# Scores and outputs read six heads where the products are written; two heads are gathered

## Chip, cores and metric

The kernel runs on one core of one Trainium2 chip. The metric is the device time of one execution in microseconds (us). TensorE (PE) multiplies, VectorE (DVE) and ScalarE (ACT) do the elementwise work, GpSimd (POOL) small elementwise work and indexed transfers, and SyncE (SP) issues most of the DMAs, one after another in a fixed order.

## Reference, cut to what matters

Inputs are float32. A gated linear attention over 4 batches, 8 heads, 768 positions and 48 channels per head feeds a mixture of experts that routes each token to one expert, and then a second layer with a maximum of three products.

```python
for t in range(S):
    ar, ai = (a_re_n[:, :, t, :, None], a_im_n[:, :, t, :, None])
    new_re = ar * S_re - ai * S_im
    new_im = ar * S_im + ai * S_re
    kv = np.einsum('bhd,bhe->bhde', k[:, :, t], v[:, :, t])
    S_re, S_im = (new_re + kv, new_im)
    y[:, :, t] = np.einsum('bhd,bhde->bhe', q[:, :, t], S_re)
...
expert_idx = np.argmax(logits, axis=1)
...
h = np.maximum(x[mask] @ w1[e], 0.0)
out[mask] = gate_w[mask, None] * (h @ w2[e])
...
h = np.maximum(np.maximum(x @ w1, x @ w2), x @ w3)
return (h @ w_out).astype(np.float32)
```

## The kernel before

The 8 x 48 = 384 channels of a batch are split into 3 groups (`G`) of 128 partitions, and the 768 positions into 6 chunks (`NCH`) of 128. The work of a batch b has two parts.

`recur` (called R below; R0 to R3) runs the complex gates through all 64 half-chunk positions of all chunks at once, in 8 blocks of 8 steps. It is a chain on DVE: two dependent instructions per step (lines 202 and 215), with the preparation of later blocks and the products filled in between. The products (lines 169, 175 and 186) go into the tile `QK`, which holds keys and queries, each with a real and an imaginary part, all multiplied by gates. There is one buffer of `QK` for all batches (`qk_p`, 1 buffer).

`chunks` (called C; C0 to C3) works on the 6 chunks of a batch. In `QK` the 48 channels of one head are spread over the partitions in such a way that TensorE can't contract over them in place. So `restack` (line 326) copies all of `QK` by DMA into tiles `KQ` of 96 partitions, where a head's 48 real and 48 imaginary channels lie below each other: 18 DMAs per batch, in pieces of 1, 2 and 3 chunks. Then, for each chunk, `scores` multiplies keys by queries for each head (line 361, tile `sc`, one matmul per head with 96 rows), DVE masks the result into `sT` (line 363), and PE transposes the keys (line 371, tile `kt`) for `state` (lines 385 and 392, tile `W`). `state` gives `Z`, which four DMAs copy into `Zs` with 96 partitions (line 412). `output` adds to `y` the product of `sT` with the values (line 427) and that of the query with the state of the earlier chunks (line 430). After that come `rows` (line 504, tile `xp`), the routing on DVE and `place` (tile `rank`), and an indexed DMA writes the token's row to its expert's list in memory.

Every matmul of float32 appears in the trace as two instructions. `sc`, `kt`, `W`, `y`, `xp` and `rank` share four PSUM buffers in turn.

The first expert layer is cut into jobs, each a list of tokens of one expert that is known to be full early: seven jobs in plain float32 (numbers 0 to 6; lines 730 and 754), and then the rest (line 621 to 623), which starts with job 7. A job reads 8 weight tiles `wr` of 384 KB. Jobs 0 to 2 need the tokens of batch 0, jobs 3 to 6 those of batches 0 and 1, job 7 those of batches 0 to 2. With `GATE = 2` the weight loads of early jobs stand behind the copies of the attention in SP's order.

The program is written in the order of `SCHED`: R0, C0, two jobs, R1, C1, two and a half jobs, R2, C2 with R3, the other early jobs, two slices of job 7, C3, the rest. A scheduler that plans with its own durations then sets the order on each engine, so DVE, PE and SP work through fixed lists in which these parts are interleaved. From about 467 us on, only the expert layers are left.

## Time and profile before

| what | us |
|---|---|
| median of 3 runs (998.87 to 1001.46) | 999.44 |
| the profiled execution, its own time | 1002.36 |
| its span in the profile | 1000.7 |
| DVE busy in the span | 593.2 |
| PE busy in the span | 821.3 |

A row of a view is one instruction group, one stretch of time or one wait; times inside the profile count from the start of the span. "PEclk" is the granted TensorE clock as a share of full speed, "DMA share" the mean busy share of the 16 DMA engines.

### The profile page before, as it was taken

Reading aid. Unit: us, or ns where it says so; the run is one execution under the profiler, and the core shown is the slowest. Engines: PE = TensorE matmul, PEld = TensorE weight load, DVE = VectorE, ACT = ScalarE, POOL = GpSimd, SP = SyncE. Lnnn points to the kernel's source line nnn. Section 1 sums busy time; section 2 is a strip of 40 time slices with the busy share of each in tenths; the row PEclk is TensorE's granted clock in tenths of the full one; section 3 lists DMA queues with packets and bytes.
Section 4 is the critical chain, followed back from the end, with each engine's and each line's share of the span. In section 5 each row is a group of like instructions: output and inputs, shape, how many; then the busy total and the mean of one; then the engine's idle time right before and its main releaser. Section 6 shows DMA issues by size and latency. Waiting matters only on the chain.

```text
span 1000.7 us, 15691 instructions
## 1 busy us (share of the span) xinstructions
PE 821.3 (82%) x5490; PEld 723.4 (72%) x5490; DVE 593.2 (59%) x1596; ACT 417.1 (42%) x1045; POOL 144.6 (14%) x230
## 2 busy tenths in 40 slices
PE   1004784769778888789899999998999999999996
PEld 1002674558656776678799999997888888888886
DVE  6989599749984895345667877785232323232222
ACT  5444466336544652335556565563121212121211
POOL 7001011100120012001312222224010101010000
PEclk9999795989788979989899999999999999999999
DMA  9835943995489639942756776662020201020001
GB/s 324 150 104 123 241 130 110 238 242 164 137 269 212 198 94 292 216 131 74 242 177 210 216 215 215 208 210 69 24 64 1 64 1 64 1 64 1 32 1 35
DMA packets 94217, 139.20 MB, mean 139 GB/s; under 512 B 26434, under 2 KB 66770, under 8 KB 94130
## 3 DMA queue, kind: packets, MB, share of 16 engines
q1 hardware_dynamic: 88018, 121.27, 44.0%
q0 software_dynamic: 6112, 16.85, 6.1%
q8 instruction: 45, 0.74, 0.3%
q14 instruction: 42, 0.34, 0.1%
HBM read 93.80 MB, written 22.36 MB: 116 GB/s over the span
## 4 chain that ended last, share of the span: by engine, by line
PE 55%; DMA 20%; DVE 17%; ACT 3%; SPq 2%; issue 2%; POOL 1%; DVEq 0%; ACTq 0%; POOLq 0%
PE h L621 10%; PE h L622 10%; PE h L623 10%; DMA wr<-wm 7%; DMA KQ<-QK 5%; PE acc L621 5%; PE acc L623 5%; PE acc L622 5%; DVE T L202 3%; DMA wt<-qk 2%; DVE T L215 2%; PE h L730 2%; PE acc L754 2%; DMA ain<-a 2%; PE xp L504 1%
## 5 line engine op out<-in xcount | busy, mean ns | idle before, releaser
L865 DVE TENSOR_TENSOR h2s<-h,h2s 128x512 f32<-128x512 f32 x72 | 49.8, 692 | 188.2 <-PE h L623 188.2
L623 PE MATMUL h<-x2h,w2l 128*128 128x512 f32 x324 | 126.6, 391 | 0.0
L622 PE MATMUL h<-x2l,w2h 128*128 128x512 f32 x324 | 126.5, 390 | 0.0
L621 PE MATMUL h<-x2h,w2h 128*128 128x512 f32 x324 | 124.4, 390 | 0.0
L202 DVE TENSOR_TENSOR T<-gates,T 128x216 f32<-128x216 f32 x256 | 97.0, 379 | 4.7 <-ACT gates L147 0.5
L614 ACT CAST h2h<-h2s 128x512 fp32r<-128x512 f32 x36 | 22.3, 620 | 145.4 <-DVE h2s L865 145.4
L730 PEld LDWEIGHTS h<-xh,wr 128*128 128x128 f32 x336 | 51.4, 224 | 36.8 <-DMA wr<-wm 27.3
L621 PE MATMUL acc<-w2h,hh 128*110 128x384 f32 (+2 forms) x200 | 69.3, 348 | 3.9 <-ACT hh L738 3.9
L615 DVE TENSOR_TENSOR w1l<-wr,w1h 128x384 fp32r<-128x384 f32 x72 | 43.7, 607 | 47.7 <-ACT w1h L614 47.5
L623 PEld LDWEIGHTS h<-x2h,w2l 128*128 128x128 f32 x324 | 60.8, 188 | 12.8
L738 ACT ACTIVATE hh<-h 128x128 f32<-128x128 f32 (+5 forms) x128 | 45.8, 359 | 57.3 <-PE h L730 43.6
L622 PEld LDWEIGHTS h<-x2l,w2h 128*128 128x128 f32 x324 | 60.8, 188 | 12.3
L541 POOL DMA_INDIRECT xs<-x,pos x24 | 25.6, 1065 | 304.0 <-DVE T L215 74.0
L730 PE MATMUL h<-xh,wr 128*128 128x128 f32 (+1 forms) x336 | 54.7, 312 | 17.8 <-DMA wr<-wm 16.8
L621 PE MATMUL h<-xh,w1h 128*128 128x330 f32 (+3 forms) x216 | 68.1, 317 | 1.3 <-ACT xh L614 1.2
L621 PEld LDWEIGHTS h<-x2h,w2h 128*128 128x128 f32 x324 | 60.7, 188 | 11.7
L324 PE MATMUL warm_s<-QK,ones 128*128 128x480 f32 x12 | 7.3, 774 | 75.1 <-DVE QK L186 75.1
L622 PE MATMUL acc<-w2l,hh 128*110 128x384 f32 (+2 forms) x200 | 67.9, 341 | 0.0
L622 PE MATMUL h<-xl,w1h 128*128 128x330 f32 (+3 forms) x216 | 67.6, 313 | 0.0
L623 PE MATMUL h<-xh,w1l 128*128 128x330 f32 (+3 forms) x216 | 67.5, 313 | 0.0
L361 PE MATMUL sc<-KQ 96*128 96x128 f32 x384 | 54.5, 294 | 13.8 <-DMA KQ<-QK 12.6
L361 PEld LDWEIGHTS sc<-KQ 96*128 96x128 f32 x384 | 49.3, 203 | 20.3 <-issue 16.6
(204 smaller groups left out, 1967.4 us busy)
## 6 DMA issues: line engine op xcount, KB each, us to landing
wr<-wm SPq DMA_DIRECT2D x128, 384.0 KB
ain<-a SPq DMA_DIRECT2D x32, 288.0 KB
KQ<-QK SPq DMA_DIRECT2D x24, 384.0 KB
w2r<-w SPq DMA_DIRECT2D x24, 384.0 KB
xs<-zero POOLq DMA_DIRECT2D x16, 384.0 KB, 10.2
KQ<-QK SPq DMA_DIRECT2D x24, 256.0 KB
wt<-qk SPq DMA_DIRECT2D x32, 144.0 KB
pl<-qk SPq DMA_DIRECT2D x32, 144.0 KB
```

The costliest lines, as they stand in the source:

```text
L202: r = tt(out=sub(To, so, [[X, 2], [PJ, 3 * GN], [1, 2]]), in0=sub(N5, j * NW, [[1, NW]]), in1=sub(T, 2 * j, [[0, 2], [PJ, 3 * GN], [1, 2]] ...
L215: r = tt(out=new, in0=new, in1=sub(M, RW + 2 * j, [[-RW, 2], [PJ, GN], [1, 2]]), op=ALU.add)
L361: k["pe"] = nc.tensor.matmul(ps[:, i], Ks[:, h], Qs[:, h], start=True, stop=True)
L541: r = nc.gpsimd.indirect_dma_start(out=self.xs_d, out_offset=bass.IndirectOffsetOnAxis(ap=pos, axis=0), in_=x, in_offset=None, bounds_chec ...
L614: nc.scalar.copy(out=hi, in_=src)
L615: nc.vector.tensor_tensor(out=lo, in0=src, in1=hi, op=ALU.subtract)
L621: r = nc.tensor.matmul(out, ah, bh, start=first, stop=False)
L622: nc.tensor.matmul(out, ah, bl, start=False, stop=False)
L623: nc.tensor.matmul(out, al, bh, start=False, stop=last)
L730: r = nc.tensor.matmul(ps, wh[:, c], xh[:, d, :n], start=d == 0, stop=d == KD - 1)
L738: r = nc.scalar.activation(out=hh[:, :n], in_=ps, func=AF.Relu)
L865: nc.vector.tensor_tensor(out=h, in0=pss[m], in1=h, op=ALU.max)
```

## The change

On the host, channels are put on other partitions: group g of the 3 now holds the 48 channels of head 2g on partitions 0 to 47 and those of head 2g+1 on partitions 64 to 111. The 16 partitions behind each of them (48 to 63 and 112 to 127) hold a third of the channels of heads 6 and 7. `scores` and `output` read heads 0 to 5 straight from `QK`, real and imaginary part in two matmuls of 48 rows that accumulate. Heads 6 and 7 are brought together by DMA into two fixed tiles `last0` and `last1` (3 chunks each). The state `Z` is read in place, so the copies `Zs` fall away. `QK` gets a second buffer, and the rules in `recur` that kept a batch's products back (`late`) fall away. The transposes take 128 partitions instead of 96. `spread` makes `E` by one multiplication and smaller DMAs.

```diff
 def host_attn(q, k, v, a_re, a_im):
+    g, p = np.arange(G)[:, None], np.arange(128)[None]
+    own, par = p % 64 < D, p // 64
+    hh, dd = np.where(own, 2 * g + par, 6 + par), np.where(own, p % 64, 16 * g + p % 64 - D)
     def dirs(x):
-        y = x.transpose(0, 3, 1, 2).reshape(B, G, 128, NCH, C)
+        y = x.transpose(0, 1, 3, 2)[:, hh, dd].reshape(B, G, 128, NCH, C)
...
-        self.qk_p = P("a_qk", 1)
-        self.s_p = P("a_stack", 2)
+        self.qk_p = P("a_qk", 2)
+        s_p = P("a_stack", 1)
+        self.last = [s_p.tile([112, 2, 2, RC * C], F32, name=f"last{i}") for i in range(NCH // RC)]
...
-            late = b > 0 and i < 3
-            p, *more = [products(x) for x in (((), (), (0, 1))[i] if late else (i - 1,) if i else ())] or [iter(())]
+            p = products(i - 1) if i else iter(())
...
-        nc.gpsimd.memset(E, 0.0)
+        nc.gpsimd.memset(E[:, 3], 0.0)
+        nc.gpsimd.tensor_scalar(out=E[:, 0:3], in0=Ed[:112], scalar1=self.k["own"][:112], scalar2=None, op0=ALU.mult)
...
-    def restack(self, b, n, QK):
...
+    def gather(self, b, QK):
+        for lo, hi in ((0, 1), (1, RC), (RC, NCH)):
+            t, o = self.last[lo // RC], lo % RC * C
+            for g in range(G):
+                for par in range(2):
                     self.k["dma"] = self.nc.sync.dma_start(
+                        out=t[64 * par + 16 * g : 64 * par + 16 * g + 16].rearrange("p x c n -> p (x c) n")[:, :, o : o + (hi - lo) * C],
+                        in_=pview(QK, 64 * par + D, (g * NCH + lo) * C, [1, 16], [[GN * C, 4], [1, (hi - lo) * C]]),
                     )
...
+        def KQ(n, x, c, pr, par):
+            if pr == 3:
+                t, cols = last(n)
+                return t[64 * par : 64 * par + D, x, c, cols]
+            return pview(QK, 64 * par, (((x * 2 + c) * G + pr) * NCH + n) * C, [1, D], [[1, C]])
...
-                    k["pe"] = nc.tensor.matmul(ps[:, i], Ks[:, h], Qs[:, h], start=True, stop=True)
+            for pr in range(4):
+                for c in range(2):
+                    for par in range(2):
+                        k["pe"] = nc.tensor.matmul(
+                            ps[par][:, pr], KQ(n, 0, c, pr, par), KQ(n, 1, c, pr, par), start=c == 0, stop=c == 1
+                        )
...
-                    k["pe"] = nc.tensor.transpose(ps[:, i * 96 : (i + 1) * 96], Ks[:, hf * 4 + i], k["ident"][:96, :96])
+                    k["pe"] = nc.tensor.transpose(ps[:, i * 128 : i * 128 + w], x, k["ident"][:w, :w])
...
-            z = Zs[n + 1] = self.c_p.tile([96, H, D], F32, tag="Zs", name="Zs" + nm(n + 1), bufs=3)
-            for c in range(2):
-                for par in range(2):
-                    nc.sync.dma_start(
...
-                            k["pe"] = nc.tensor.matmul(o, Zf[:, h * D : h * D + m], Qs[:, h], start=False, stop=True)
+            for pr in range(4 if n else 0):
+                for c in range(2):
+                    for par in range(2):
+                        k["pe"] = nc.tensor.matmul(
+                            y[64 * par : 64 * par + D, pr], Z[n][64 * par : 64 * par + D, pr, c], KQ(n, 1, c, pr, par),
+                            start=False, stop=pr == 3 and c == 1,
+                        )
...
-SPLITS = ([(0,1),(1,3)],[(0,3)])
```

The order on the engines changes too. First DVE around the end of R3, where `QK3` is batch 3's tile, `sT_3_0_0` the masked scores of batch 3, chunk 0, and `w1l_7_0_0` the first weight slice of job 7. Before:

```order
L186 TENSOR_TENSOR QK3_2921<-qe3_2922,T_86 128x72
...
L615 TENSOR_TENSOR w1l_7_0_0_4127<-wr_7_0_0_4124,w1h_7_0_0_4126 128x384
L615 TENSOR_TENSOR w2l_7_0_0_4131<-wr_7_0_0_4124,w2h_7_0_0_4130 128x384
...
L363 TENSOR_TENSOR sT_3_0_0_4213<-sc_3_0_0_4208,mask_249 128x512
L363 TENSOR_TENSOR sT_3_0_1_4220<-sc_3_0_1_4215,mask_249 128x512
```

After:

```order
L195 TENSOR_TENSOR QK3_3052<-qe3_3053,T_86 128x72
...
L631 TENSOR_TENSOR w1l_7_0_0_4320<-wr_7_0_0_4317,w1h_7_0_0_4319 128x384
L631 TENSOR_TENSOR w2l_7_0_0_4324<-wr_7_0_0_4317,w2h_7_0_0_4323 128x384
L631 TENSOR_TENSOR w1l_7_0_1_4344<-wr_7_0_1_4341,w1h_7_0_1_4343 128x384
L631 TENSOR_TENSOR w2l_7_0_1_4348<-wr_7_0_1_4341,w2h_7_0_1_4347 128x384
L378 TENSOR_TENSOR sT_2_4_0_3703<-sc_2_4_0_3685,mask_253 128x512
L378 TENSOR_TENSOR sT_2_4_1_3705<-sc_2_4_1_3686,mask_253 128x512
```

C3 came directly behind R3; now chunks 4 and 5 of C2 stand between them.

Next PE where C3 begins, with `acc_6`, `h_4` and so on the matmuls of jobs 6 and 4. Before, all early jobs are through:

```order
L754 MATMUL acc_6_0_0_4020<-wr_6_0_6_4074,hh_6_0_6_4080 128x384
L730 MATMUL h_6_0_7_4085<-xh_6_0_4008,wr_6_0_7_4083 128x128 x3
L679 MATMUL xT_7_0_0_4110<-ident_171,xt_7_0_4105 128x120 x3
L679 MATMUL xT_7_0_1_4116<-ident_171,xt_7_0_4105 128x120 x3
L754 MATMUL acc_6_0_0_4020<-wr_6_0_7_4083,hh_6_0_7_4089 128x384
L361 MATMUL sc_3_0_0_4208<-KQ_3_0_4178 128x128 x4
L361 MATMUL sc_3_0_1_4215<-KQ_3_0_4178 128x128 x4
```

After, half of job 4 stands ahead of C3, and jobs 5 and 6 are mixed into its chunks 0 to 2:

```order
L520 MATMUL xp_2_5_4037<-idE_306,yT_2_5_4006 128x120 x4
L746 MATMUL h_4_0_4_4083<-xh_4_0_2658,wr_4_0_4_4081 128x128 x3
...
L372 MATMUL sc_3_0_0_4400<-QK3_3052 128x128
L372 MATMUL sc_3_0_1_4401<-QK3_3052 128x128
...
L746 MATMUL h_5_0_0_4132<-xh_5_0_4117,wr_5_0_0_4130 128x128 x3
L746 MATMUL h_5_0_1_4140<-xh_5_0_4117,wr_5_0_1_4138 128x128 x3
L372 MATMUL sc_3_0_1_4401<-last0_93 128x128
```

So two and a half jobs moved from ahead of C3's first scores to behind R3's end, and the two score tiles are filled in turn.

Last SP's list at the same place; `wr_6_0_7` is a weight tile of job 6, `v_3_2` the values of batch 3, chunk 2. Before:

```order
L333 DMA KQ_3_0_4178<-QK3_2921 16x16x128
L698 DMA wr_6_0_7_4083<-wm 128x768
L333 DMA KQ_3_0_4178<-QK3_2921 16x16x128 x5
L333 DMA KQ_3_0_4178<-QK3_2921 16x16x256 x6
L774 DMA x1_61<-x1o_6_0_0_4093 128x384
L333 DMA KQ_3_3_4199<-QK3_2921 16x16x384 x6
L698 DMA wr_7_0_2_4799<-wm 128x768
```

After:

```order
L714 DMA wr_7_0_0_4317<-wm 128x768
L714 DMA wr_7_0_1_4341<-wm 128x768
L339 DMA last0_93<-QK3_3052 16x4x128 x3
...
L339 DMA last0_93<-QK3_3052 16x4x256 x6
...
L366 DMA v_3_2_4534<-vs 128x384
L339 DMA last1_94<-QK3_3052 16x4x384 x6
L714 DMA wr_7_0_2_5054<-wm 128x768
L714 DMA wr_7_0_3_5084<-wm 128x768
L714 DMA wr_5_0_0_4130<-wm 128x768
```

The 18 copies remain 18, each a quarter of the size, and the weights of jobs 5 and 6 moved behind them.

## Rows read from the trace of the kernel before

**Rows 1.** Busy time by engine, from the page.
```profile
PE 821.3 (82%) x5490; PEld 723.4 (72%) x5490; DVE 593.2 (59%) x1596; ACT 417.1 (42%) x1045; POOL 144.6 (14%) x230
```
**Rows 2.** Windows: stretch, length, busy time by engine, granted clock, DMA share, GB/s.
```profile
0.00:88.00 88.00, 2.98 (x15) 2.92 (x15) 72.58 (x230) 39.24 (x100) 21.03 (x100) 1.00 0.65 175
88.00:183.00 95.00, 71.22 (x612) 58.96 (x612) 81.03 (x269) 50.96 (x141) 11.18 (x17) 0.78 0.66 165
183.00:304.00 121.00, 94.38 (x771) 75.25 (x770) 90.74 (x299) 60.90 (x178) 13.92 (x23) 0.87 0.81 212
304.00:389.00 85.00, 71.59 (x680) 60.67 (x680) 70.05 (x237) 44.78 (x128) 7.09 (x8) 0.92 0.72 187
389.00:467.00 78.00, 63.56 (x644) 53.70 (x643) 27.13 (x77) 26.40 (x75) 7.53 (x11) 0.93 0.70 165
467.00:1000.70 533.70, 517.57 (x2778) 471.86 (x2776) 251.63 (x489) 194.78 (x426) 83.82 (x74) 0.99 0.32 101
```
**Rows 3.** The same view, three stretches inside R1, R2 and R3.
```profile
135.00:182.00 47.00, 31.48 (x261) 27.10 (x260) 45.31 (x158) 26.91 (x76) 7.19 (x10) 0.71 0.45 127
225.00:267.00 42.00, 35.86 (x407) 31.93 (x406) 40.10 (x145) 27.29 (x76) 5.46 (x6) 0.91 0.53 152
328.00:367.00 39.00, 32.65 (x387) 28.24 (x386) 38.27 (x135) 24.23 (x66) 4.13 (x4) 0.94 0.52 151
```
**Rows 4.** DVE's waits from 88 to 389 us: total, times, longest.
```profile
DVE sT L363 <- PE sc L361: 21.3, 8, 5.1
DVE QK L169 <- DMA wr<-wm: 10.2, 2, 8.0
```
**Rows 5.** PE in order of time, one chunk of C3: start, length, instructions.
```profile
444.40 1.16 PE L385 MATMUL W<-v,KT 128*64 128x48 f32 x32
445.49 0.90 PE L392 MATMUL W<-Z,ident 112*112 112x384 f32 x2
446.32 0.43 PE L427 MATMUL y<-sT,v 128*64 128x128 f32 x4
446.58 0.39 PE L430 MATMUL y<-KQ,Zs 96*48 96x128 f32 x4
446.81 0.39 PE L427 MATMUL y<-sT,v 128*48 128x128 f32 x4
447.91 0.39 PE L430 MATMUL y<-KQ,Zs 96*48 96x128 f32 x4
448.23 2.05 PE L361 MATMUL sc<-KQ 96*128 96x128 f32 x16
450.11 0.82 PE L371 MATMUL kt<-ident,KQ 96*128 96x96 f32 x8
450.77 0.17 PE L531 MATMUL rank<-OH,trib 128*128 128x8 bf16 x1
451.06 1.15 PE L504 MATMUL xp<-idE,yT 112*128 112x120 f32 x8
452.14 0.68 PE L385 MATMUL W<-v,KT 128*64 128x48 f32 x16
456.17 2.05 PE L361 MATMUL sc<-KQ 96*128 96x128 f32 x16
```
**Rows 6.** PE in order of time, two slices of an early job.
```profile
384.72 0.83 PE L730 MATMUL h<-xh,wr 128*128 128x128 f32 x6
385.39 0.81 PE L754 MATMUL acc<-wr,hh 128*128 128x384 f32 x2
386.04 0.83 PE L730 MATMUL h<-xh,wr 128*128 128x128 f32 x6
```
**Rows 7.** The chain that ended last, behind R3's end and later: start, length.
```profile
398.86 10.62 DMA KQ<-QK
418.20 12.38 DMA wr<-wm
604.24 3.68 DMA wr<-wm
```

More of the change, by code (lines that the diff above doesn't have):

```diff
@@ L87, in __init__ @@
         self.T = n_p.tile([128, 6, 3 * GN, JB, 2], F32, name="T")
-        self.qk_p = P("a_qk", 1)
-        self.s_p = P("a_stack", 2)
+        self.qk_p = P("a_qk", 2)
+        s_p = P("a_stack", 1)
+        self.last = [s_p.tile([112, 2, 2, RC * C], F32, name=f"last{i}") for i in range(NCH // RC)]
+        for t in self.last:
+            self.nc.gpsimd.memset(t[32:64], 0.0)
         self.c_p = P("a_chunk", 2)
@@ L259, in recur @@
             n2 = norms[i + 2] if i + 2 < NBLK else iter(())
-            late = b > 0 and i < 3
-            p, *more = [products(x) for x in (((), (), (0, 1))[i] if late else (i - 1,) if i else ())] or [iter(())]
-            queue += [take(n1, 2), take(n2, 1), take(p, 1), take(n1, 1), take(p, 1), n1, p, *more]
+            p = products(i - 1) if i else iter(())
+            queue += [take(n1, 2), take(n2, 1), take(p, 1), take(n1, 1), take(p, 1), n1, p]
             after = THR.get(b, {}).get(i)
@@ L342, in chunks @@
         QK, Ed = self.out[b]
-        st = [self.restack(b, 0, QK)]
+        self.gather(b, QK)
+        last = lambda n: (self.last[n // RC], slice(n % RC * C, (n % RC + 1) * C))
         E = self.spread(b, Ed)
-        st += [self.restack(b, n, QK) for n in range(RC, NCH, RC)]
-        KQ = lambda n, x: st[n // RC][:, :, x, n % RC * C : (n % RC + 1) * C]
-        V, S, KTs, Z, Zs, yT = {}, {}, {}, {}, {}, {}
+        def KQ(n, x, c, pr, par):
[3 more added lines that the diff above has]
+            return pview(QK, 64 * par, (((x * 2 + c) * G + pr) * NCH + n) * C, [1, D], [[1, C]])
+        V, S, KTs, Z, yT = {}, {}, {}, {}, {}
         nm = lambda n: f"_{b}_{n}"
@@ L352, in scores @@
         def scores(n):
[L353 removed]
             V[n] = self.c_p.tile([128, DM], F32, tag="v", name="v" + nm(n), bufs=3)
             nc.sync.dma_start(V[n], v_d[b, n])
[L356 to L363 removed]
+            ps = [k["ps_m"].tile([128, 4, C], F32, tag="am", name=f"sc{nm(n)}_{par}") for par in range(2)]
+            for pr in range(4):
[4 more added lines that the diff above has]
+                        )
+            S[n] = []
+            for par in range(2):
+                s = self.c_p.tile([128, 4, C], F32, tag="sT", name=f"sT{nm(n)}_{par}", bufs=4)
+                nc.vector.tensor_tensor(out=s, in0=ps[par], in1=sub(k["mask"], 0, [[0, 4], [1, C]]), op=ALU.mult)
                 S[n].append(s)
@@ L366, in scores @@
                 return
-            KT = KTs[n] = self.c_p.tile([128, H, 2, D], F32, tag="KT", name="KT" + nm(n), bufs=1)
+            KT = KTs[n] = self.c_p.tile([128, 8, 112], F32, tag="KT", name="KT" + nm(n), bufs=1)
             for hf in range(2):
@@ L370, in scores @@
                 for i in range(4):
-                    k["pe"] = nc.tensor.transpose(ps[:, i * 96 : (i + 1) * 96], Ks[:, hf * 4 + i], k["ident"][:96, :96])
-                nc.scalar.copy(
-                    out=KT[:, hf * 4 : hf * 4 + 4].rearrange("p h c d -> p (h c d)"), in_=ps[:, 0:DM]
-                )
+                    g, c = divmod(4 * hf + i, 2)
+                    if g < G:
+                        x, w = sub(QK, ((c * G + g) * NCH + n) * C, [[1, C]]), 128
+                    else:
+                        t, cols = last(n)
+                        x, w = t[:, 0, c, cols], 112
+                    k["pe"] = nc.tensor.transpose(ps[:, i * 128 : i * 128 + w], x, k["ident"][:w, :w])
+                nc.scalar.copy(out=KT[:, 4 * hf : 4 * hf + 4], in_=sub(ps, 0, [[128, 4], [1, 112]]))
         def state(n):
@@ L1182, in body @@
             k["mask"] = mask_tile(nc, cp)
+            const("own", [128, 1])
+            nc.vector.tensor_reduce(out=k["own"], in_=sub(k["ident"], D, [[64, 2], [1, 16]]), axis=AX.XY, op=ALU.add)
+            nc.vector.tensor_scalar(out=k["own"], in0=k["own"], scalar1=-1.0, scalar2=1.0, op0=ALU.mult, op1=ALU.add)
             const("tau", [128, 1])
```

43 lines of the change are left out of this document (12 added, 31 removed).

## The prediction

> **What bounds the kernel now.** I read the busy times first [rows 1]: PE leads with 821.3 us, but that is an average over stages. So I cut the span by stages [rows 2], at the ends of the DVE chains of R0, R1 and R3 (88, 183, 389 us), at the first copy for C2 (304) and at C3's last `xp` (467). The reader should compare PE and DVE in each line. From 467 us on PE is busy 517.57 of 533.70 us with the expert layers. The change touches nothing there, so I leave these 533.70 us as they are and ask only when that stage begins.
>
> Ahead of it no engine is full. From 88 to 389 us DVE is busy 81.03 + 90.74 + 70.05 = 241.8 of 301 us [rows 2]: 59 us are waits. They are not spread evenly. In the middle of each batch [rows 3] DVE is busy 45.31 of 47, 40.10 of 42 and 38.27 of 39 us, which is 96, 95 and 98%. The waits lie between these stretches, where a batch's copies `KQ` and weight tiles move. Two kinds are named [rows 4]: `sT` waits for scores (21.3 us), and a product waits behind weight loads (10.2 us). So in R1 to R3 the bound is the DVE chain plus the copies that hold it up. Behind R3's end, from 389 to 467 us, it is another one: first DMA (a piece of the copy takes 10.62 us, later a weight tile 12.38 us behind the copies [rows 7]), then PE, whose chunk follows chunk without a gap, 7.94 us apart (448.23 to 456.17 [rows 5]). PE is busy 63.56 of these 78 us.
>
> **The change part by part. First the time of R3's end.** With two `QK` buffers a batch's products no longer wait for the copy of the batch before. Scores of heads 0 to 5 need no copy, and those of heads 6 and 7 a quarter of the bytes. So I take both kinds of waits in [rows 4] as gone. What is left for DVE is its work. Of the 241.8 us some 6.5 us (chunks 4 and 5 of C2: four masks, one state, four chunks' routing, at the share that they have in these stretches) now stand behind R3's end in DVE's list. The remaining 235 us at 96% [rows 3] take 245 us; R3 would end at 88 + 245 = 333 us. The new order has two waits of its own. R3's first product has to wait until C1's last output on PE has read the other `QK` buffer, and early weight loads stand among R's own loads in SP's list. I add 4 us, between nothing and the 10.2 us of the load wait in [rows 4]. That gives **337 us instead of 389**: 52 us gained there.
>
> **Then what PE still has to do at that time.** This takes most of it back. PE's lists are fixed, and the order shows that at R3's end PE has not only C3 ahead of it as before, but also two chunks of C2 and two and a half jobs.
>
> The price of a chunk after the change comes from [rows 5], start to start. `sc`: 16 instructions in 1.88 us (448.23 to 450.11), 0.118 us each. `kt` 0.66, `rank` 0.29, `xp` 1.08, `W` 1.09 + 0.83. `y` takes 1.91 us for 32 instructions; its groups of four start 0.22 us apart (446.58 to 447.91 is six of them), that is 0.055 us per instruction, half of what `sc` shows: two instructions that write to different halves of the columns run side by side.
> - `sc` becomes 32 instructions of 48 rows, in pairs on partitions 0 to 47 and 64 to 111. No row of this trace shows two matmuls on different rows side by side. From below, a pair costs one instruction (0.11 us): 1.9 us as now. From above two: 3.7 us. I take the lower end, because the nearest row, `y`, shows full overlap of pairs on different columns.
> - `y` keeps its first 16 instructions (0.9 us), but the second part becomes 32 of 48 rows and 48 columns: 1.8 us if pairs overlap (0.9 before), 3.5 if not. I take 1.8.
> - `kt` goes from 96 to 128 columns: 0.66 x 128/96 = 0.88 us.
> - Changes between kinds of matmul cost: the last four of `y` start at 447.91 and `sc` at 448.23, 0.32 us instead of 0.22. So a change costs 0.1 us. In the new list there are 228 such changes ahead of the second layer instead of 90, and 66 instead of 23 inside C3.
>
> The Trainium skill says in "TensorEngine Tiling (Array Packing)", Key Properties, that changing the tiling mode, not just the tile, drains TensorE. The 0.1 us agrees; the rule speaks against this change, which more than doubles the number of such changes. By the row the 43 more in C3 are 4.3 us, and they are in the sum; if changes of mode were free, the sum would end 4.3 us earlier, at 983 us.
>
> Together a middle chunk takes 7.94 + 0.22 + 0.9 + 0.2 = 9.3 us. The work left on PE at 337 us:
> - rest of C2 (from chunk 4's transposes to the last `xp`: three `y`, one `sc`, one `W`, four `xp`, and two short waits for the copy of `y`): **20 us**;
> - two and a half jobs: a slice takes 1.32 us (384.72 to 386.04 [rows 6]), eight and the transposes 10.8, so **27 us**;
> - C3: chunk 0 3.9, chunk 1 5.7, chunks 2 to 4 3 x 9.0 without the changes of mode among jobs, chunk 5 6.2, the two last outputs 6.9: 50, and 3 for the changes of mode among the jobs: **53 us**;
> - job 7's first two slices and transposes, as before: **5 us**.
>
> That is 105 us, against 63.56 us busy before in the same stage. Waits come on top. Directly behind R3's end DVE's list has job 7's first weights, whose load is released by R3's end: a load of its own takes 3.68 us [rows 7], and conversion follows; queued behind them on DVE are the masks of C2's chunk 4, and PE then stands for want of PSUM. I take 6 us. Later SP's list holds job 5's first weights behind the values and the copy for chunks 3 to 5, which wait for C2's last output: three to four loads behind each other, of which C2's last `xp` and half of job 4 cover about half. I take 5 us, between nothing and the 12.38 us that such a load took behind the copies [rows 7]. Further 2 us for copies out of PSUM. Sum of waits: **13 us**, where 78 - 63.56 = 14.4 us were idle before.
>
> **The sum.** 337 + 105 + 13 = 455 us for C3's last `xp`, instead of 467: 12 us less. The later stage is unchanged. In the profiled execution 1002.36 - 12 = 990.4 us. The median of the runs is 2.9 us below the profiled time, so I predict **987 us**.
>
> Edits that I cost at nothing: the copies `Zs` that fall away are off PE's path in most chunks, and the price above has no wait for them. `E` is now made on POOL, which is busy 7.09 of 85 us [rows 2] and has the first state's transposes to hide behind; without that cover it would be one small instruction per batch, under 1 us. The two extra DVE instructions at the start lie ahead of R0's chain, less than 0.5 us. ACT copies 448 instead of 384 columns per partition of `KT`; it is busy 26.4 of 78 us [rows 2].
>
> **Rivals.**
> 1. *DVE gets full and little is late behind it.* R3 ends at 88 + 235/0.98 = 328 us (the best stretch in [rows 3]), PE's 105 us follow with 4 us of waits: 437, so 30 us gained, 969 us. For it: DMA has far less to move. Against: each list is planned with durations that differ from the chip's, and lists wait for each other.
> 2. *Pairs on different rows don't run side by side (slower).* Then a score tile costs 1.8 us more and an output 1.7. Behind R3's end there are 7 of the first and 8 of the second: +26 us, and PE would hold up R2 and R3 too, by some 10 us: 491 us, +24 us, about 1023 us. It decides from a small value on: 240 pairs lie behind R3's end, so the 12 us are lost when a pair takes 0.05 us more than an instruction alone, 0.16 us.
> 3. *Only the pairs of the output are serial.* Both of them write to one PSUM bank, on partitions 0 to 47 and 64 to 111. 8 x 1.7 = 14 us more, C3 ends at 469: no change, about 1001 us. For `y`'s pairs on different columns, which also write to one bank, [rows 5] shows overlap, which speaks against it. The Trainium skill says, in "TensorEngine Tiling (Array Packing)", Gotcha 1, that different row tiles cannot access the same PSUM bank at the same time; these pairs differ in rows and in columns, and no run here shows which counts.
> 4. *The recurrence doesn't get faster.* DVE's fixed list has masks and products that wait for PE, and PE is now fuller. If that costs as much as the `sT` waits do now (21.3 us [rows 4]), R3 ends at 354, and 354 + 113 = 467: no change, 999 us, with some chance to be a little slower.
>
> **How the numbers follow.** My forecast (975 to 996 us) gets 0.47, rival 1 0.19, rival 2 0.12, rival 3 0.09, rival 4 0.13. Within 0.3% (3 us, about what a measurement of this kernel can tell from no change) lie most of rivals 3 and 4: 0.12. Slower are rival 2 and the other part of 3 and 4: 0.21. Faster are the forecast and rival 1, and a little of 4: 0.67. The range from 964 to 1006 us takes in the forecast, rivals 1, 3 and 4 and leaves out rival 2. The forecast's own range is 975 to 996.
>
> **What would show it.** R3's last product (the last DVE instruction into `QK`) at about 337 us; DVE over 93% busy from 88 us to there. `sc` 32 instructions in about 1.9 us, and `y` 48 in about 2.9. C3's last `xp` at about 455. DVE standing for `w1l` behind R3's end for about 6 us. The stage behind it 533 us long, as now. Wrong would be: a score tile that takes 3.5 us; R3 ending behind 350; job 5's weights late by more than 10 us; or a later stage that changes its length.

## The result, and the profile after

The changed kernel takes 1007.99 us (median of 6 runs, 1002.89 to 1009.18) against 999.33 us for the kernel before (6 runs). The ratio is 1.0074, 95% interval 1.0045 to 1.0103: it is slower by 0.7%, and 2 us above the end of my range. The profiled execution took 1008.53 us, its span 1006.8.

First its stages, cut as in [rows 2] but at its own ends of R0 to R3 (88, 174.5, 258.4, 352.9 us) and at C3's last `xp` (472.9). The columns are the same.

```profile
88.00:174.50 86.50, 68.31 (x731) 55.78 (x731) 80.42 (x262) 49.85 (x134) 14.20 (x17) 0.85 0.40 118
174.50:258.40 83.90, 75.02 (x700) 60.33 (x700) 78.22 (x251) 49.62 (x143) 9.09 (x15) 0.85 0.58 170
258.40:352.90 94.50, 83.74 (x715) 64.62 (x710) 76.70 (x251) 44.95 (x128) 8.97 (x15) 0.84 0.49 144
352.90:472.90 120.00, 113.71 (x1267) 93.19 (x1267) 37.80 (x120) 41.45 (x114) 13.62 (x18) 1.00 0.41 124
472.90:1006.80 533.90, 516.55 (x2779) 470.83 (x2777) 252.01 (x489) 194.72 (x426) 83.51 (x74) 0.99 0.32 101
```

R3 ends at 352.9 us, 36 us earlier than before, and C3 ends 6 us later. The stage behind it is as long as it was. Look at R3: R1 and R2 take 86.5 and 83.9 us, R3 takes 94.5 for no more work on DVE.

The same view over the whole part from 94 us, where C0 begins, to C3's last `xp`: first the kernel before, then the changed one.

```profile
94.00:466.90 372.90, 294.65 (x2691) 245.65 (x2691) 263.23 (x861) 179.55 (x510) 37.19 (x53) 0.87 0.73 185
```
```profile
94.00:472.90 378.90, 334.83 (x3394) 271.09 (x3393) 267.42 (x861) 182.40 (x510) 39.89 (x58) 0.89 0.47 139
```

PE's busy time rose from 294.65 to 334.83 us (+40.2), and its idle time fell from 78.2 to 44.1 us (-34.2). The difference is the 6 us. DVE's total hardly moves.

DVE's waits from 88 to 353 us in the changed kernel (total, times, longest), to be held against [rows 4]. The first line is one of the kernel before that [rows 4] leaves out, the rest are the changed kernel's:

```profile
DVE y L130 <- ACT y L126: 13.6, 6, 6.4
```

```profile
DVE sT L378 <- PE sc L372: 10.1, 5, 4.9
DVE q L553 <- PE rank L548: 3.9, 2, 2.3
DVE t L421 <- ACT Z L414: 3.3, 4, 1.1
DVE L L524 <- ACT x L522: 2.1, 2, 1.6
```

The wait behind weight loads is gone, as I said, and so is, but for 0.5 us, the larger one of `y` for ACT, which I had not named. The wait of masks for scores has halved; I had taken it as gone. Together with the small ones DVE stands for 29.6 of these 265 us.

One chunk of C3 on PE in order of time, as in [rows 5]:

```profile
441.32 1.61 PE L372 MATMUL sc<-QK 48*128 48x128 f32 x24
442.76 0.61 PE L372 MATMUL sc<-last 48*128 48x128 f32 x8
443.30 0.87 PE L392 MATMUL kt<-ident,QK 128*128 128x128 f32 x6
444.01 0.36 PE L392 MATMUL kt<-ident,last 112*128 112x112 f32 x2
...
447.85 1.09 PE L436 MATMUL y<-sT,v 128*64 128x128 f32 x16
448.87 1.51 PE L443 MATMUL y<-QK,Z 48*48 48x128 f32 x24
450.21 0.60 PE L443 MATMUL y<-last,Z 48*48 48x128 f32 x8
450.75 1.61 PE L372 MATMUL sc<-QK 48*128 48x128 f32 x24
```

Scores take 1.98 us (441.32 to 443.30) for 32 instructions, transposes 0.91, the output 2.90 (447.85 to 450.75), the chunk 9.43 (and the next one 9.30). My prices of a chunk were right. They hold where PE has nothing but chunks.

Last, the place where R3 loses its 10 us: four stretches of R3 in the window view.

```profile
258.40:278.00 19.60, 13.41 (x160) 11.69 (x155) 14.16 (x50) 8.58 (x21) 5.88 (x10) 0.83 0.40 105
278.00:300.00 22.00, 19.28 (x83) 13.56 (x83) 14.99 (x53) 8.54 (x27) 2.17 (x2) 0.61 0.62 173
300.00:320.00 20.00, 20.00 (x154) 15.31 (x153) 16.96 (x47) 11.37 (x35) 0.00 (x0) 1.00 0.70 220
320.00:352.90 32.90, 31.04 (x324) 24.06 (x321) 30.59 (x102) 16.46 (x47) 0.93 (x3) 0.91 0.34 100
```

Until 278 both engines stand in turn. From 278 to 320 PE is busy for 39.3 of 42 us, at first at a granted clock of 0.61, and DVE for 32.0. The first stretch is the end of C1, alone on PE:

```profile
258.59 1.61 PE L372 MATMUL sc<-QK 48*128 48x128 f32 x24
260.03 0.61 PE L372 MATMUL sc<-last 48*128 48x128 f32 x8
260.57 0.18 PE L547 MATMUL rank<-OH,trib 128*128 128x8 bf16 x1
260.61 0.37 PE L548 MATMUL rank<-carry,ones 128*128 128x8 f32 x2
260.84 1.13 PE L520 MATMUL xp<-idE,yT 112*128 112x120 f32 x8
267.44 1.97 PE L436 MATMUL y<-sT,v 128*64 128x128 f32 x16 [5.47 <-DVE sT L378]
```

C1's last scores come only behind R2's end. The output that follows them belongs to the chunk before, whose masks DVE made at 249.69 and 250.43 us. But `rank` and `xp` have taken two of the four PSUM buffers, so by their turn this output needs the one that holds the first of the last scores, and it starts when DVE has masked them. DVE's list has R3's first steps ahead of that mask:

```profile
266.70 0.68 DVE L378 TENSOR_TENSOR sT<-sc,mask 128x512 f32<-128x512 f32 x1
```

PE works in the order of its list, has only this one `xp` to do meanwhile, and waits 5.47 us. The slices of job 2 (a slice is a job's work on one of its 8 weight tiles), which need batch 0 alone, come later in the list, from 278.93 on and among the scores of C2's first chunk. PE begins these scores at 287.59 and ends them at 301.5; DVE's longest wait ends there:

```profile
301.38 0.69 DVE L378 TENSOR_TENSOR sT<-sc,mask 128x512 f32<-128x512 f32 x1 [4.91 <-PE sc L372]
```

### The profile page after: what moved, and what is told of

Its sections match the earlier page's. It is cut to its first block, busy times and chain, and to the rows that moved or that the text cites. A ratio compares the mean times of both kernels' runs of the same rounds, so it can differ in the third digit from the quotient of the medians.

```text
span 1006.8 us, 16912 instructions
## 1 busy us (share of the span) xinstructions
PE 860.2 (85%) x6194; PEld 747.6 (74%) x6194; DVE 598.0 (59%) x1598; ACT 419.8 (42%) x1045; POOL 152.9 (15%) x236
## 3 DMA queue, kind: packets, MB, share of 16 engines
q1 hardware_dynamic: 57554, 104.16, 34.2%
## 4 chain that ended last, share of the span: by engine, by line
PE 65%; DVE 19%; DMA 8%; ACT 3%; issue 2%; POOL 1%; SPq 1%; DVEq 0%; ACTq 0%; POOLq 0%
PE h L637 10%; PE h L638 10%; PE h L639 10%; PE acc L637 5%; PE acc L638 5%; PE acc L639 5%; DVE T L211 5%; PE sc L372 4%; PE acc L770 4%; PE h L746 4%; DMA wr<-wm 3%; DVE T L224 3%; DMA wt<-qk 2%; PE y L443 2%; PE W L404 2%
## 5 line engine op out<-in xcount | busy, mean ns | idle before, releaser
L224 DVE TENSOR_TENSOR T<-T 128x72 f32<-128x72 f32 x256 | 58.9, 230 | 4.0
L331 PEld LDWEIGHTS warm_s<-QK,ones 128*128 128x128 f32 x12 | 2.8, 246 | 77.6 <-DVE QK L195 74.7
L746 PEld LDWEIGHTS h<-xh,wr 128*128 128x128 f32 x336 | 48.6, 209 | 14.5 <-issue 3.8
L631 DVE TENSOR_TENSOR w2l<-wr,w2h 128x384 fp32r<-128x384 f32 x72 | 43.4, 602 | 25.9 <-ACT w2h L630 25.6
```

The source lines that it names most:

```text
L224: r = tt(out=new, in0=new, in1=sub(M, RW + 2 * j, [[-RW, 2], [PJ, GN], [1, 2]]), op=ALU.add)
L631: nc.vector.tensor_tensor(out=lo, in0=src, in1=hi, op=ALU.subtract)
L746: r = nc.tensor.matmul(ps, wh[:, c], xh[:, d, :n], start=d == 0, stop=d == KD - 1)
```

## Experiments

Ratios are to the kernel before on the same chip. "Idle" is PE's from 94 us to C3's last `xp`, "R1, R2, R3" the length of each in us.

| run | median, us | ratio (95%) | R1, R2, R3 | last xp | PE busy + idle |
|---|---|---|---|---|---|
| before | 999.33 | 1 | 95.3, 105.4, 100.6 | 466.9 | 294.7 + 78.2 |
| changed | 1007.99 | 1.0074 (1.0045 to 1.0103) | 86.5, 83.9, 94.5 | 472.9 | 334.8 + 44.1 |
| e1 half the state part | 993.92 | 0.9924 (0.9897 to 0.9950) | 83.7, 84.5, 83.9 | 456.2 | 317.4 + 44.8 |
| e2 jobs 1, 2 behind C3 | 1019.53 | 1.0184 (1.0153 to 1.0214) | 85.0, 85.3, 83.5 | 463.2 | 312.4 + 56.8 |
| e3 jobs 5, 6 behind C3 | 1005.83 | 1.0063 (1.0034 to 1.0093) | 84.9, 84.0, 94.9 | 447.2 | 311.2 + 42.0 |
| e4 unused matmuls, 3 x 16 | 1022.20 | 1.0212 (1.0178 to 1.0245) | 84.5, 81.6, 92.6 | 489.3 | 355.4 + 39.9 |
| e8 unused matmuls, 2 x 8 | 1013.41 | 1.0117 (1.0085 to 1.0148) | 86.4, 81.6, 98.3 | 480.2 | 347.7 + 38.5 |
| e5 pairs apart | 1049.20 | 1.0487 (1.0455 to 1.0520) | 81.5, 86.4, 108.0 | 515.7 | 403.8 + 17.9 |
| e6 one buffer | 1063.70 | 1.0618 (1.0576 to 1.0659) | 123.7, 127.4, 124.3 | 530.2 | 330.2 + 106.0 |
| e7 routing first | 1024.39 | 1.0235 (1.0198 to 1.0271) | 93.5, 109.6, 84.8 | 484.4 | 332.4 + 58.0 |
| e9 slices between chunks | 985.10 | 0.9872 (0.9834 to 0.9909) | 84.9, 81.5, 87.6 | 455.5 | 313.9 + 47.6 |
| e10 e9 and e3 together | 987.90 | 0.9897 (0.9859 to 0.9935) | 86.4, 81.6, 89.5 | 434.5 | 292.7 + 47.8 |
| e11 slices in blocks | 1013.58 | 1.0163 (1.0118 to 1.0207) | 84.7, 79.9, 106.6 | 480.8 | 322.3 + 64.5 |
| e12 before, jobs 5, 6 behind C3 | 1014.79 | 1.0173 (1.0133 to 1.0213) | 94.0, 105.1, 101.0 | 456.3 | 274.9 + 87.4 |
| e13 before, slices between | 1012.71 | 1.0106 (1.0056 to 1.0157) | 94.3, 95.3, 94.3 | 477.4 | 286.4 + 97.0 |
| e14 spread, no tie | 989.59 | 0.9880 (0.9833 to 0.9926) | 84.6, 84.7, 85.0 | 455.1 | 328.4 + 32.7 |
| e15 e9, fewer ahead of C3 | 990.38 | 0.9887 (0.9831 to 0.9944) | 86.4, 81.6, 79.6 | 453.7 | 310.5 + 49.2 |
| e16 spread in C2 alone | 1004.40 | 1.0030 (1.0006 to 1.0054) | 84.9, 84.0, 85.7 | 467.4 | 332.0 + 41.4 |
| e17 spread in C1 alone | 995.60 | 0.9951 (0.9921 to 0.9982) | 86.4, 85.4, 83.4 | 460.9 | 331.0 + 35.9 |

Above everything that I had expected for them came e4, e7, e13, e15 and e16, below it e9 and e10; e2 and e17 miss a range by less than 1 us, and e5 lies between its two.

**What bounds the part ahead of C3's last `xp`: work on PE, order, or clock.** Theory A is that PE's work sets the pace, B that the fixed order of DVE's list does, C that the halved clock costs the time. Five kernels take work from PE or add some.

e1, in the state part of the output:

```diff
-                for c in range(2):
+                for c in range(1):
```

e2, in the list of jobs (batch, expert, first token, number of tokens, whether plain); e3 makes `(2, 5, 0, 240, False)` and `(2, 6, 0, 240, False)` of the entries of experts 5 and 6 in the same way (e2 also has 8 instead of 16 slices ahead of R1, all that are left there):

```diff
-EARLY = [(0, 0, 0, 96, True), (0, 1, 0, 96, True), (0, 2, 0, 96, True), (1, 3, 0, 128, True), (1, 4, 0, 128, True), (1, 5, 0, 128, True), (1, 6, 0, 128, True), (2, 7, 0, 240, False)]
+EARLY = [(0, 0, 0, 96, True), (1, 3, 0, 128, True), (1, 4, 0, 128, True), (1, 5, 0, 128, True), (1, 6, 0, 128, True), (2, 1, 0, 240, False), (2, 2, 0, 240, False), (2, 7, 0, 240, False)]
```

e4 and e8:

```diff
-WARM0 = {0:(0,6)}
+WARM0 = {0:(0,6), 1:(0,16), 2:(0,16), 3:(0,16)}
+WARM0 = {0:(0,6), 1:(0,8), 2:(0,8)}
```

> The changed kernel, but the output's state part uses the real parts alone: 16 instead of 32 matmuls (y from QK and Z) in each of the 20 chunks that have a state; that part of the output is left out. In the changed kernel's trace these 32 take 1.88 us in a chunk of C3 (448.87 to 450.75), so 0.94 us of PE's work goes per chunk, 18.8 us in all; 13 such chunks lie ahead of R3's end (352.9 us there) and 7 behind it. Theory A, PE's work is now what sets the pace (PE is busy 49.85 of the 50 us from 290 to 340, where DVE stands for scores): R3's last product comes 8 to 12 us earlier, at 341 to 345 us, C3's last xp 15 to 19 us earlier, and the kernel takes 989 to 994 us. Theory B, the fixed order of DVE's list and not the amount of work on PE sets R3's end: it stays at 350 to 353 us, only the 7 chunks behind it count, 6.6 us, and the kernel takes 1000 to 1003 us. Theory C, the halved clock right behind PE's idle stretches (0.5 from 186.5 to 200.2 and from 282 to 299 us) is what costs: the clock's pattern stays, R3's end moves by less than 4 us, about 998 to 1000 us.

> The changed kernel, but experts 1 and 2 have no early job; 240 of their tokens each become a job of the stage behind C3. Two plain jobs of 96 tokens, 10.8 us each with their transposes by the rows of before, go from PE's lists ahead of R3's end (they lie among the chunks of C1 and C2), and 192 tokens are added behind. Theory A, PE's work sets the pace: R3's last product comes 10 to 18 us earlier, at 335 to 343 us, C3's last xp 18 to 24 us earlier, at 449 to 455; the stage behind gets 13 to 20 us longer for the tokens and the second tiles; in all 1000 to 1008 us. Theory B, the order sets R3's end: it stays at 350 to 353, C3's last xp stays at 470 to 473, and the added work makes 1020 to 1027 us.

> The changed kernel, but experts 5 and 6 have no early job; 240 of their tokens each become a job of the stage behind C3. These are the two jobs that stood among C3's chunks. Both theories expect PE's work behind R3's end to fall by 21.6 us and 2 to 3 us of changes of mode: C3's last xp at 447 to 451 instead of 472.6 us. The later stage takes 256 tokens more, 16 to 24 us. If the tokens cost the same there, 1004 to 1008 us and nothing is gained; if a token costs less there because PE needs three passes instead of four, 998 to 1003 us. Theory C (the clock): the same.

> The changed kernel, but with 16 matmuls of 480 columns on the constant tile at the beginning of C1, C2 and C3 too, about 3.2 us each at the high clock and 6.4 at the low; their results aren't used. They begin when the batch's last product is written, while PE has little to do (176 to 187 and 259 to 272 us in the changed kernel). Theory C, the halved clock behind these stretches costs the time (0.5 from 186.5 to 200.2 us and from 282 to 299 us, while PE is busy 10 of 10 us): the granted clock stays at 1.0 there, R3's last product comes 6 to 12 us earlier and the kernel takes 996 to 1002 us. Theory A, PE's work sets the pace: the added 48 matmuls cost 5 to 15 us, of which the stretches in which PE stood anyway hide half; 1008 to 1016 us. Theory B: no change, 1006 to 1010 us.

> The changed kernel with 8 unused matmuls of 480 columns at the beginning of C1 and C2 only (0.8 us each, 12.8 us more on PE). With 16 at C1, C2 and C3 the halved clock fell from 82 to 51 us between 88 and 480 us, R3's end came at 345.1 instead of 352.9 us, and the kernel took 14 us more with 38.4 us more work, of which the 12.8 us at C3 lay wholly on the path. Theory C (the halved clock behind idle stretches costs time): without the matmuls at C3 and with half of the others, R3's end at 343 to 348, C3's last xp at 466 to 470, the kernel 1001 to 1005 us. Theory A, with the clock counting for nothing: 12.8 us more work, at most 6 us hidden: 1011 to 1017 us.

In e1 17.5 us less on PE bring C3's last `xp` 16.7 us forward, with the idle time unchanged: as theory A said, except that 10.6 us of it came in R3 alone and nothing in R2. In e2 R3 shrinks too, but PE idles 13 us more; half of what was taken is lost. In e3 the work taken stood behind R3's end, R3 keeps its 94.9 us, and the later stage gives back 21.8 of 25.7 us. So the amount of work counts, but not everywhere, and something particular happens in R3.

Theory C isn't settled. A block of 16 unused matmuls takes 13.5 to 15.6 us, some four times what I had put down. The three blocks of e4 take 44.6 us (15.52 + 15.57 + 13.54) and raise PE's busy time by 20.6 us only, at a mean clock of 0.94 instead of 0.89: the rest of PE's work got 24 us shorter (one row, from 94 us to C3's last `xp`):

```profile
94.00:489.30 395.30, 355.40 (x3480) 273.47 (x3477) 268.28 (x856) 183.30 (x509) 43.28 (x56) 0.94 0.46 133
```

Bought with matmuls that do nothing, it still costs 14 us. A high clock alone didn't make R3 short: in e4 it is 0.96 there, and R3 takes 92.6 us with a block of 15.6 us in it. e8 raised the mean clock to 0.90 only and says little.

**The two parts of the change.** e5 has the two heads of a pair one behind the other, e6 takes the second buffer away.

```diff
-            for pr in range(4):
-                for c in range(2):
-                    for par in range(2):
+            for par in range(2):
+                for pr in range(4):
+                    for c in range(2):
...
-        self.qk_p = P("a_qk", 2)
+        self.qk_p = P("a_qk", 1)
```

e5 does the first in both places; e6 has the second and the rules of `late` as in the kernel before.

> The changed kernel, with the two heads of a pair one after the other instead of in turn: in scores and in the state part of the output the loop over par is the outer one, so neighbours in PE's list use the same 48 rows. Same work, same number of instructions. In the changed kernel's trace a pair of scores begins 6 to 7 ns apart and the next pair 105 ns later (102 ns for the output). If that is two matmuls running side by side, each instruction alone takes 0.10 to 0.105 us: a chunk's scores rise from 1.98 to 3.4 us, the state part from 1.88 to 3.2, in all 24 x 1.4 + 20 x 1.35 = 61 us more on PE. Theory A (the part ahead of C3's last xp takes PE's busy time and some 40 us of idle time): C3's last xp at 525 to 540 instead of 472.6, the kernel 1060 to 1075 us. Theory B (DVE's order sets R3's end, only the 8 score tiles and 10 state parts behind it count): 25 us more, 1030 to 1036 us. If pairs never ran side by side: no change, 1008 us.

> The layout alone: the changed kernel with one buffer of QK and the rules that kept a batch's products back. The scores and outputs now read QK itself, so a batch's products wait until the last output of the batch before has read it, not only until its copies are made. Theory A: PE's work ahead of C3's last xp stays near 335 us (a few less, since jobs no longer lie among the chunks), but its idle time goes from 44 us to at least the 78 us of the kernel before, and with the longer hold of QK to about 100: C3's last xp at 505 to 530 and the kernel at 1040 to 1065 us. If the second buffer gave little: below 1015 us.

The rows of e5 in C3, in order of time, answer to those of the changed kernel above:

```profile
484.48 1.60 PE L372 MATMUL sc<-QK 48*128 48x128 f32 x12
...
487.91 0.87 PE L392 MATMUL kt<-ident,QK 128*128 128x128 f32 x6
...
492.02 1.09 PE L436 MATMUL y<-sT,v 128*64 128x128 f32 x16
493.04 1.51 PE L443 MATMUL y<-QK,Z 48*48 48x128 f32 x12
...
496.26 1.60 PE L372 MATMUL sc<-QK 48*128 48x128 f32 x12
```

Scores now take 3.43 instead of 1.98 us (484.48 to 487.91), the state part 3.22 instead of 1.88 (493.04 to 496.26). So in the changed kernel the pairs do run side by side, the scores' and the output's. The added 69 us cost 43, between theories A and B, since 26 us went into idle time. Without the second buffer (e6) each R takes 124 to 127 us and PE idles 106: the new layout can't do without it.

**Where the slices of jobs stand.** e7 forces the routing ahead of the next R's last block. e9 writes the jobs in turn with C1 and C2 and ties each chunk's first scores behind the slices written before; e11 has the tie alone, e14 the turn alone. e10 adds e3's edit to e9 (the 16 slices that are then left stand in C2's turn); e12 and e13 do to the kernel before what e3 and e9 do to the changed one; e15 has 28 instead of 20 slices in C2's turn; e16 and e17 spread one group each.

The tie, and what it needs in the jobs:

```diff
                             ps[par][:, pr], KQ(n, 0, c, pr, par), KQ(n, 1, c, pr, par), start=c == 0, stop=c == 1
                         )
+                        if k.get("job"):
+                            issue_order(self.tc, k["pe"], k.pop("job"))
...
                     r = nc.tensor.matmul(acc[s][:tw], hh[:, c], wh, start=f == 0, stop=f == NF - 1)
                     gate(r)
+                    k["job"] = r
```

The turn (e9, e13 and e14), and below it those of e16 and e17, and e7's edit:

```diff
-SCHED = [[("R0",)], [("C0",)], [("P", 16)], [("R1",)], [("C1",)], [("P", 20)], [("R2",)], [("C2",), ("R3",)], [("P",)], "L", [("L", 2)], [("C3",)], [("L", 6)]]
+SCHED = [[("R0",)], [("C0",)], [("R1",)], [("C1",), ("P", 24)], [("R2",)], [("C2",), ("R3",), ("P", 20)], [("P",)], "L", [("L", 2)], [("C3",)], [("L", 6)]]
+SCHED = [[("R0",)], [("C0",)], [("P", 16)], [("R1",)], [("C1",)], [("R2",)], [("C2",), ("R3",), ("P", 20)], [("P",)], "L", [("L", 2)], [("C3",)], [("L", 6)]]
+SCHED = [[("R0",)], [("C0",)], [("R1",)], [("C1",), ("P", 16)], [("P", 20)], [("R2",)], [("C2",), ("R3",)], [("P",)], "L", [("L", 2)], [("C3",)], [("L", 6)]]
...
-THR = {}
+THR = {1: {7: 5}, 2: {7: 5}}
```

> The changed kernel, with the whole routing of a batch ahead of the last of the eight blocks of the next recurrence in DVE's list (THR for R1 and R2). In the changed kernel's trace PE is idle for 18 us of the 86 us of R1, because C0's last rank stands behind R1's products on DVE (PE waits 7.42 us for OH there) and jobs 0 and 1 need C0's tokens; here job 0 stands ahead of C1 in PE's list. Theory A (busy time of PE and its idle time): 6 to 12 us of idle time are filled with slices of jobs that now mix less with C1: C3's last xp at 460 to 467, the kernel 996 to 1003 us. Theory B (DVE's list sets R's ends): C0's routing ahead of R1's last block makes R1 3 to 8 us later, and what PE gains is lost: 1004 to 1012 us.

> The changed kernel with the slices of early jobs between the chunks instead of inside them: the first scores of a chunk stand behind the job slices written before it, and the jobs are written in turn with C1 and with C2 (24 and 20 slices, 12 ahead of C3). In the changed kernel's trace the scores among job slices (R2: 160 instructions) take 0.104 us each from start to start, 0.075 among chunks alone (C3), and each change of kind costs; summed over 90 to 480 us the changes take some 10 us more than in the kernel before. Theory A (PE's work plus some 40 us of idle time): the work falls by 6 to 10 us, C3's last xp at 462 to 467, the kernel 997 to 1003 us. Theory B (DVE's list sets R's ends): slices between chunks keep masks waiting, R3's last product at 353 or later and the kernel 1006 to 1020 us.

> As the run with slices between the chunks, and the jobs of experts 5 and 6 behind C3 as well, so that no early job stands behind R3's end. Moved alone, these jobs took 25.7 us off C3's last xp and put 21.8 us onto the later stage. Theory A: both add up: C3's last xp at 437 to 443, the later stage 555 us, the kernel 992 to 999 us, level with the kernel before or a little under it. Theory B: 1002 to 1015 us.

> The changed kernel with only the tie that keeps a chunk's scores behind the job slices written before it: all early jobs of a batch then stand in one block between two batches of chunks (16 slices ahead of C1, 20 ahead of C2, 20 ahead of C3). Changes of kind on PE are fewest. Theory A: the work falls by 8 to 12 us, but at each block C's masks and outputs wait for 13 to 26 us, which R can cover only as far as its products have their own buffer: about 1000 to 1012 us. Theory B: R3's last product at 360 or later, above 1012 us.

> The kernel before, with the jobs of experts 5 and 6 moved behind C3 and nothing else: what that move is worth without the new layout. There PE has 78 us of idle time ahead of C3's last xp, and these jobs filled some of it. If busy time counts only where PE is full, C3's last xp comes 0 to 8 us earlier while the later stage gets 21.8 us longer: 1013 to 1022 us. If every job moved is worth as much as in the changed kernel (25.7 us): 995 to 998 us.

> The kernel before with the same edit as the run with slices between the chunks (jobs written in turn with C1 and C2, the first scores of a chunk behind the slices written before it). Its scores are matmuls of 96 rows of the same kind as the jobs' own, so a slice among them costs nothing extra (0.112 us per score instruction in every stage of its trace), and PE has 78 us of idle time ahead of C3's last xp. If the interleaving costs the new layout alone: 994 to 1006 us. If the edit is simply a better order for either kernel: 982 to 990 us.

> The changed kernel with the jobs written in turn with C1 and C2 (24 and 20 slices), without the tie: slices are spread over all chunks of a batch but still stand inside the scores. If a slice inside a chunk's scores is what costs (changes of kind, pairs torn apart): C3's last xp at 466 to 474 and the kernel 1000 to 1010 us. If only the crowding of the jobs into the first three chunks cost: as with the tie, 983 to 990 us.

> The kernel with slices between the chunks, with 28 instead of 20 slices in turn with C2, so that 4 instead of 12 are left ahead of C3. In the run with 20, PE is busy 74 of the 88 us of R3; eight slices of 1.32 us are 10.6 us. If PE's idle time in R3 takes them: R3's last product 0 to 4 us later, C3's last xp 6 to 10 us earlier, 975 to 981 us. If R3 gets longer by what they take: 984 to 988 us.

> The changed kernel with only the second group of job slices (20, written ahead of C2) written in turn with C2 and R3; the first group (16) stays ahead of R1 and C1. Theory D (the loss is made in R3, where the slices crowd into C2's first three chunks, PE is busy all of the time and DVE waits): R3 lasts 83 to 87 instead of 94.5 us, its last product comes at 341 to 346, C3's last xp at 455 to 464, the kernel takes 988 to 998 us. Theory C (halved clock, in R2 as much as in R3): half of the gain, 997 to 1003 us. If both groups count: the same half.

> The changed kernel with only the first group of job slices (16) written in turn with C1; the second group (20) stays ahead of R2 and C2 as one piece. Theory D (the loss is made in R3): R2 stays at 82 to 86 us, R3 at 92 to 97, C3's last xp at 468 to 474, the kernel 1003 to 1010 us. If both groups count: 996 to 1002 us.

e7 lost, by more than either theory had allowed: R1 and R2 get longer by 7 and 26 us. e9 is the find: 985.1 us, faster than both kernels. Its stages, R1 to R3, then from R3's end to C3's last `xp`:

```profile
88.50:173.40 84.90, 69.52 (x731) 55.89 (x731) 80.49 (x262) 49.91 (x134) 14.26 (x17) 0.85 0.37 101
173.40:254.90 81.50, 69.95 (x736) 56.42 (x736) 78.54 (x253) 50.63 (x144) 9.10 (x16) 0.88 0.62 186
254.90:342.50 87.60, 73.95 (x756) 59.51 (x755) 76.14 (x254) 47.03 (x133) 11.33 (x16) 0.92 0.53 163
342.50:455.50 113.00, 105.86 (x1186) 86.79 (x1186) 35.43 (x116) 39.22 (x108) 11.99 (x16) 1.00 0.43 132
```

Among DVE's waits up to R3's end the largest group is 3.9 us, and the masks' wait for scores, 10.1 us in the changed kernel, is this row:

```profile
DVE sT L380 <- PE sc L372: 0.2, 1, 0.2
```

Two things have changed. A chunk's scores in R2 are cheaper: first the changed kernel, then e9, PE's busy time in line 372 between R1's and R2's end.

```profile
174.50:258.40 83.90, 17.50 (x160) 0.85 0.58 170
```
```profile
173.40:254.90 81.50, 14.06 (x192) 0.88 0.62 186
```

That is 3.5 us on average for the 32 of a chunk, with slices among those of two of the five chunks, against 2.3 us without, at a mean clock of 0.85 and 0.88. And all 192 score instructions of C1's six chunks now lie ahead of R2's end, where the changed kernel had 160, so that the end of C1 no longer stands alone at the beginning of R3.

I expected e14 to show that the slices' standing inside the scores is what costs. It didn't: without the tie, spread over all chunks, the kernel is as fast (0.9880, intervals overlap), though the scores in R2 are as dear as in the changed kernel (3.5 us for 32):

```profile
171.90:256.60 84.70, 20.33 (x186) 0.84 0.60 176
```

From 94 us to C3's last `xp`, first e9, then e14:

```profile
94.00:455.50 361.50, 313.87 (x3398) 256.18 (x3397) 265.31 (x863) 183.31 (x510) 41.18 (x59) 0.92 0.49 146
94.00:455.10 361.10, 328.37 (x3395) 264.31 (x3394) 265.05 (x859) 182.94 (x510) 40.83 (x56) 0.91 0.50 146
```

PE has 14.5 us more work in e14 than in e9 and 14.9 us less idle time. So the tie saves work that turns into idle time, and what counts is that the slices are spread: with the tie alone, in blocks (e11), R3 takes 106.6 us.

e16 and e17 were to show that the loss is made by the slices in R3. That fell as well. In e16 R3 is as short as hoped (85.7 us), but nine slices moved behind its end. A slice has six `h` instructions (line 746); from R3's end to C3's last `xp` there are 120 of them in the changed kernel and 174 in e16:

```profile
352.90:472.90 120.00, 17.07 (x120) 1.00 0.41 124
```
```profile
341.20:467.40 126.20, 24.85 (x174) 1.00 0.50 152
```

In e17 even more slices crowd R3, 23 instead of 20 (138 `h` instructions), and R3 is short all the same, now that C1's scores are through by then. The granted clock in R3 is 0.98, where the changed kernel has 0.84 (the windows of R2 and R3):

```profile
175.50:260.90 85.40, 76.89 (x774) 62.82 (x775) 80.56 (x265) 51.35 (x145) 10.05 (x17) 0.84 0.58 166
260.90:344.30 83.40, 80.13 (x767) 61.69 (x765) 74.81 (x246) 47.91 (x137) 9.11 (x13) 0.98 0.61 188
```

R3's length goes with C1's end in the other runs with two buffers too. Where at least 186 of C1's 192 score instructions lie ahead of R2's end (e1, e2, e7, e9, e10, e14, e15, e17), R3 takes 79.6 to 89.5 us; where 160 or fewer do (the changed kernel, e3, e4, e5, e8, e11), 92.6 to 108.0. e16, with 160 and nine slices fewer, takes 85.7.

C3's last `xp` comes 5.5 us earlier in e16 and 12.0 in e17, 17.8 with both (e14). So the two groups seem to add up, with two thirds from the one ahead of C1; e14 and e9 also write 8 slices more in C1's turn (24 instead of 16), and no run has both groups spread without that. The kernel before gains nothing from the same edits (e13 1.1% slower, e12 1.7%): there PE has 78 us of idle time, and e13 has 97. So the place of the slices is a loss that comes with the new layout, as far as e13, which has the turn and the tie together, can show it. (Its expectation has 0.112 us per score instruction in every stage of the kernel before; by the windows of line 361 it is 0.134 to 0.155 us of busy time, 12.84 to 14.84 us for 96.) e10 and e15 add nothing to e9; what they take off the part ahead of C3's end or off R3 comes back behind it (554.1 us of later stage in e10, 120.0 us from R3's end on in e15).

## Why the prediction was wrong, step by step

**The step that failed** is R3's end: "So I take both kinds of waits in [rows 4] as gone. What is left for DVE is its work.", at 96%, 337 us. DVE's work was right: 235.4 us from 88 to 353. But it took 265 us, 89%, and R3 ended at 352.9: DVE stood for 29.6 us, where I had 14 (4% of waits and 4 us). The wait for weight loads went; the masks' wait for scores stayed at half (10.1 us) and smaller waits for PE and ACT came on top. I had worked out that a chunk costs 1.4 us more, and that changes of kind more than double, and used both prices only behind R3's end. Of the 24 chunks' scores 16 lie ahead of R3's end, where I let DVE alone set the pace.

What the runs show in its place is that the order of the slices on PE makes DVE wait. Written in one piece ahead of C1 and C2, they stand among the first chunks, C1's last scores come behind R2's end, PE stands for 5.47 us there, and then, at a granted clock of 0.61, its slices hold up the scores of C2's first chunk, for which DVE waits 4.91 us. With the slices spread R3 ends at 342.5 (e9), 341.6 (e14) and 344.3 us (e17): 8.6 to 11.3 of the 15.9 us come back, and the masks' wait for scores is 0.2, 1.2 and 5.5 us. Which waits make up the rest is not traced.

That the place of the slices is worth 17.4 us at C3's end is shown by e9, e14, e16 and e17. How these 17.4 us divide into the gap at R3's beginning, dearer scores and the clock is not: e9 has less work, e14 less idle time, and both end at the same time. The clock can be much of it. By the mean clocks from 94 us to C3's last `xp` (0.89, 0.92, 0.91) the halved clock took, as an estimate, 42 us in the changed kernel, 29 in e9 and 33 in e14. So at most some 13 us in e9 and 9 in e14 are the clock's, less where PE stood anyway.

**What PE still has to do at R3's end**: predicted 105 us of work and 13 of waits, 118; measured 120.0, of which 113.7 busy. Of the 8.7 us of busy time too few 4.9 are one chunk: behind R3's end stand 256 score instructions, two chunks' more than C3's, where I counted one, and four more outputs instead of three (1.98 + 2.90 us). The other 3.8 are not traced. The waits were overestimated, 6.3 us instead of 13. Directly behind R3's end DVE stood 2.8 us for `w1l` (predicted 6), and PE stood only 0.4 us for masks; for weights of early jobs PE stood 2.8 us (predicted 5):

```profile
DVE w1l L631 <- ACT w1h L630: 2.8, 2, 2.1
PE h L746 <- DMA wr<-wm: 2.8, 1, 2.8
```

**The sum.** The profiled execution took 1008.5 us where I had 990.4. Of these 18.1 us R3's end is 15.9, the work behind it 8.7, the waits there take off 6.7, and the later stage adds 0.2. The median lies 0.5 us below the profiled time instead of 2.9, which makes the 21 us between 987 and 1008.

**Prices of a chunk**: `sc` 1.98 (1.9), `y` 2.90 (2.9), `kt` 0.91 (0.88), the chunk 9.30 to 9.43 us (9.3). **The later stage**: 533.9 us (533.7).

**Rivals.** 1, DVE full, is refuted: 89%. 2 and 3, serial pairs, are refuted by the trace and by e5. 4, DVE's list waits for PE, was right in kind: it put R3's end at 354, 1 us off. That it came so close is luck, since it took the masks' whole wait of 21.3 us as staying, and 10.1 stayed, with others beside it. Its time, 999, was too low because its 113 us behind R3's end were 120. With the slices spread the forecast's numbers come out: C3's last `xp` at 455.5 us (455) and 985.1 us (987) in e9. But that is another order than the one I predicted, and two misses cancel in it: R3 ends at 342.5 us instead of 337, and 113.0 us follow instead of 118. I didn't see that this order of the jobs would not let the gain come out.

## What to carry to other kernels

When a change trades waiting on one engine for work on another, add up the second engine's work and idle time over the whole part of the program, in every stage, not only where that engine is the last to finish: here +40 of work against -34 of idle time was the answer. And when a stage loses its idle time, look again at filler work that had been placed to fill it: the same slices in the same number cost 2% in the wrong place, while the kernel before gained nothing from moving them.
